# A three-stage kernel on one core: zeros for the places past the first 384 of each expert only, 8 transfers in place of 24

## The chip, the cores and the metric

One core of a Trainium2 chip. The time is device microseconds (us) of one execution of the whole program; lower is better. The engines are TensorE (PE: matmuls; PEld: its weight loads), VectorE (DVE), ScalarE (ACT), GpSimd (POOL) and SyncE (SP). SP and POOL issue the DMA transfers of this kernel, each on a queue of its own; 16 DMA engines carry both.

## What is computed

Attention with landmarks, then a dense feed-forward layer, then a layer of eight experts of which each token takes two. Cut to what matters:

```python
# attention: q, k, v are (4, 8, 576, 64); 32 landmarks are means over 18 rows
A, Bm, C = sm(q, k_lm), sm(q_lm, k_lm), sm(q_lm, k)
Z = ...                      # six steps towards the inverse of Bm
x = (A @ Z @ C @ v)          # laid out as (2304 tokens, 512)
# feed-forward
h = x @ w_in                 # (2304, 2048)
x = (h * np.tanh(np.log1p(np.exp(h)))) @ w_out
# experts
noisy = x @ w_gate + np.log1p(np.exp(x @ w_noise)) * noise
top2 = np.argpartition(-noisy, 2, axis=1)[:, :2]     # with softmax weights top2_w
for e in range(8):
    for k in range(2):
        mask = top2[:, k] == e
        out[mask] += top2_w[mask, k, None] * (np.maximum(x[mask] @ w1[e], 0) @ w2[e])
```

## The kernel before

**Stages.** Attention goes by the 4 batches (`attention`). The feed-forward layer goes by 8 units of 288 tokens, two to a batch. A unit has 8 steps (`hidden`): 12 matmuls into `ps_h` (L733), the nonlinear function on ACT and DVE (among it L753, L763 and L771 on DVE), and 24 matmuls with `w_out` into `ps_acc` (L788 to L790). Since `w_in` is folded into the attention's small matrices (`fold`, L700), batch b's units need batch b's attention, whose last step on TensorE is L568. While a batch's units run, the next batch's attention runs between them: `kT` and `qT` are loaded and summed to landmarks `kl` and `ql` by DVE (L327), multiplied on TensorE (L356, L390), transposed (L470, L474), multiplied with `v` (L486) and put through six small steps (L548).

**Routing.** When a unit is done, `route` copies it to `yT` (ACT), computes the gate (36 pairs of matmuls, L866 before and L864 after the change), finds each token's two experts and its place in each, and scatters the token's row (512 values and 4 of bookkeeping, 2064 bytes) to `slots` in DRAM (L1012, POOL). Each expert has a list of `CAP` = 640 places there: a first part of `CAPA` = 384 and a second of `CAPB` = 256. The expert stage then loads blocks of 128 places (`gather`), 384 or 256 to a job, multiplies them and adds the results to `out` by the token's number. For a place past the expert's count the number is set out of bounds (`entries`, L1082), so nothing is written for it.

**The zeros.** `zeros` waits until the third step of unit 0 is planned (`downed[2]`), clears a tile `zero` and writes it over all 8 x 640 places by DMAs on POOL's queue (`fill`, L282), in three sets: places 0 to 287, 288 to 575 and 576 to 639 of each expert, 8 transfers to a set. After each set an event `filled[i]` is set, and the routing of units 0, 1 and 2 waits for one each in the plan. Later it clears `out` with six more transfers. On the chip, the scatters wait for the fills that stand ahead of them, as both write `slots`.

**What sets the order.** Every engine and queue does its instructions in the order in which they are written. That order comes from a planner that runs while the kernel is built (`Order`): the parts are generators that ask for an engine with a cost, for a transfer with its bytes, or wait for events; an engine takes, of the requests that are ready, the one with the earliest due time (`DU`). The planner keeps one clock for all transfers, so bytes taken away move the planned times of all later loads, and with them the order on every engine.

**Other traffic.** While unit 0 runs, SP loads, in the order of the plan: `w_out` in pieces of 512 KB (`raw`, split by DVE in L599 to L603 and L662, two buffers in turn, so that a piece is asked for when DVE is done with the one two before), `win` (parts of `w_in` for the next batch's fold), `kT`, `qT` and the two pieces of `v`.

Of the kernel before, what the change touches and what calls it, by code (L numbers as in the profile page):

```python
# [19 lines left out]
NTOK, D = 2304, 512  # L20
DFF, NE, DFE = 2048, 8, 1024
U = 288
# [4 lines left out]
CAPA, CAPB = 384, 256  # L27
CAP = CAPA + CAPB
# [3 lines left out]
LW = 4  # L32
# [154 lines left out]
def op(engine, cost, late=0.0):  # L187
    return ("op", engine, cost, late)


def wait(event):
    return ("wait", event)


def get(ring, n=1):
    return ("get", ring, n)
# [18 lines left out]
class Kern:  # L215
# [589 lines left out]
    def zeros(self):  # L805


        yield wait(self.downed[2])
        tk = yield get(self.r_raw)
        zero = self.wp.tile([128, D + LW], F32, name="zero", tag="raw", bufs=2)  # L810
        yield op("V", 0.2)
        self.V.memset(zero, 0.0)
        slots = self.slots[: NE * CAP].rearrange("(e c) x -> e c x", e=NE)
        for i, c in enumerate(range(0, CAP, U)):
            n = min(U, CAP - c)
            for e in range(NE):
                dst = slots[e, c : c + n].rearrange("(n p) x -> p n x", p=min(n, 96))
                src = zero[: min(n, 96)].unsqueeze(1).broadcast_to([min(n, 96), max(n // 96, 1), D + LW])
                yield from self.fill(dst, src, n * 4 * (D + LW))
            self.o.set(self.filled[i])  # L820
        yield wait(self.downed[20])
        rows = self.out.rearrange("(p n) x -> p n x", p=128)
        for n in range(0, NTOK // 128, 3):
            yield from self.fill(rows[:, n : n + 3], zero[:, :D].unsqueeze(1).broadcast_to([128, 3, D]), 786432)
        self.o.put(self.r_raw, tk)
        self.o.set(self.zeroed)

    def route(self, u, acc, ta):
# [25 lines left out]
        sent, rr, trr = Event(), [], []  # L854
        o.spawn(send(), due_hidden(8 * u + 7) + DU["send"])
        yield wait(self.routed[u - 1] if u else self.emptied)
        if u < len(self.filled):
            yield wait(self.filled[u])
        tg = yield get(self.r_g)
        lg = self.bank()  # L860
        yield op("T", 0.9)
        for b in range(3):
            for c in range(4):
                for q in range(3):  # L864
                    n = 32 * (3 * b + q)
# [404 lines left out]
    def run_all(self):  # L1270
# [13 lines left out]
        self.got_wo, self.upped, self.downed = events(range(NF)), events(range(nh)), events(range(nh))  # L1284
        self.folded, self.emptied, self.zeroed, self.x_open, self.y_open, self.m_open, self.last_h = (Event() for _ in range(7))
        self.routed_a = Event()
        self.filled = [Event() for _ in range(0, CAP, U)]
        self.AT, self.WT, self.win, self.gt = {}, {}, {}, {}
        for name in ("AT", "WT", "win", "gt", "mw", "x", "yp"):
            setattr(self, "t_" + name, {})  # L1290
# [87 lines left out]
        def now(gen):  # L1378

            try:  # L1380
                while True:
                    next(gen)
            except StopIteration as r:
                return r.value


        with last:
            n_it = nc.values_load(self.nrounds[0:1, 0:1], min_val=0, max_val=(NROUND - 1) * NE)  # L1388
            with tc.For_i(0, n_it) as i:
                for p, n in ((0, CAPA), (1, CAPB)):  # L1390
                    row = i * CAP + (NE * CAP + p * CAPA)
                    of = lambda t: t.rearrange("p r e -> p (r e)")[:, bass.ds(i, 1)]
                    lw, off, _ = now(self.entries(row, p * CAPA // 128, n // 128, of(self.exps), of(self.left), "x%d" % p))
                    x = now(self.gather(row, n, Event()))
# [61 lines left out]
```

## Time and profile before

| | us |
|---|---|
| three runs | 962.16, 966.08, 966.98 |
| median | 966.08 |
| profiled execution | 968.66 |
| its span, first to last instruction | 966.8 |
| TensorE busy in it | 914.0 |
| POOL busy in it | 136.4 |

The profile records one execution. A busy TensorE is work in flight: matmuls follow each other at shorter distances than a single one lasts. The profile names for each idle time what ended it. Transfers show as issues (on SP's or POOL's queue) and as the share of the 16 DMA engines that each queue's packets took; in that view q1 is SP's queue and q0 is POOL's. The rows on which the prediction rests stand further below.

### The profile page before, as it was taken

The page shows a single profiled execution, that of the slowest core. Times are in us where ns is not written, and L with a number is a line of the kernel's source. Part 1 is how long each engine was busy: PE and PEld are TensorE (multiplying, and loading weights), DVE is VectorE, ACT ScalarE, POOL GpSimd, SP SyncE. Part 2 cuts the span into 40 slices and gives each one's busy share as a digit, 9 for nine tenths or more (in the row PEclk, how much of TensorE's full clock was granted, in tenths as well). Part 3 has the DMA queues.
Part 4 walks back from the last instruction along what each step waited for, and adds up shares of the span by engine and source line. Part 5 has one row for each costly group of instructions (what it writes and reads, how often), then busy time and mean ns, then how long its engine had stood idle before and what let it go on. Part 6 is the DMA issues. An engine that isn't in the chain of part 4 may idle for free. (4 is left out here: it accounts for less than half of the span.)

```text
span 966.8 us, 18134 instructions
## 1 busy us (share of the span) xinstructions
PE 914.0 (95%) x7135; PEld 799.1 (83%) x7135; DVE 625.7 (65%) x1519; ACT 457.6 (47%) x825; POOL 136.4 (14%) x129
## 2 busy tenths in 40 slices
PE   9979768999999998999999989999999999999995
PEld 7767656878886877889898979899989899999984
DVE  6999689566986669486958466646565555445411
ACT  2247655667766686588853233333333223323210
POOL 0002100223101200202020412101121011111102
PEclk9989989999999999999999999999999999999998
DMA  8677950565406410323243667666556355464103
GB/s 303 198 256 255 360 209 3 152 192 173 194 7 200 164 53 2 115 67 86 58 153 91 153 191 162 148 169 143 135 118 158 109 111 125 98 165 94 17 3 51
DMA packets 70075, 131.62 MB, mean 136 GB/s; under 512 B 13696, under 2 KB 34784, under 8 KB 69984
## 3 DMA queue, kind: packets, MB, share of 16 engines
q1 hardware_dynamic: 56960, 96.16, 32.6%
q0 software_dynamic: 13024, 34.25, 15.1%
q8 instruction: 58, 0.95, 0.4%
q14 instruction: 33, 0.27, 0.1%
HBM read 91.94 MB, written 39.48 MB: 136 GB/s over the span
## 5 line engine op out<-in xcount | busy, mean ns | idle before, releaser
L1151 PE MATMUL ps_up<-xh,mw 128*128 128x256 f32 (+1 forms) x1024 | 265.5, 312 | 2.8 <-ACT mw L1039 2.1
L1151 PEld LDWEIGHTS ps_up<-xh,mw 128*128 128x128 f32 x1024 | 183.1, 189 | 15.5 <-ACT mw L1039 2.5
L1160 ACT ACTIVATE gh<-ps_up 128x384 fp32r<-128x384 f32 (+1 forms) x128 | 56.1, 438 | 285.7 <-PE ps_acc L1173 161.6
L1162 DVE SCALAR_TENSOR_TENSOR gl<-ps_up,gh 128x384 fp32r<-128x384 f32 (+1 forms) x128 | 62.7, 490 | 170.1 <-ACT gh L1160 169.9
L788 PE MATMUL ps_acc<-gh,wo 128*128 128x288 f32 x512 | 159.2, 311 | 5.3 <-ACT gh L768 5.0
L1151 PE MATMUL ps_up<-xl,mw 128*128 128x384 f32 (+1 forms) x512 | 159.3, 311 | 0.0
L789 PE MATMUL ps_acc<-gl,wo 128*128 128x288 f32 x512 | 153.2, 299 | 2.8 <-DVE gl L771 2.8
L790 PE MATMUL ps_acc<-gh,wo 128*128 128x288 f32 x512 | 152.7, 298 | 0.2 <-DVE wo L662 0.2
L733 PE MATMUL ps_h<-ah,gt 128*128 128x288 f32 x512 | 127.3, 306 | 15.7 <-ACT mh L746 15.2
L1172 PE MATMUL ps_acc<-mw,gh 128*128 128x512 f32 x320 | 126.5, 395 | 0.0
L1173 PE MATMUL ps_acc<-mw,gh 128*128 128x512 f32 x320 | 126.4, 395 | 0.0
L1174 PE MATMUL ps_acc<-mw,gl 128*128 128x512 f32 x320 | 125.8, 393 | 0.0
L1185 POOL DMA_INDIRECT out<-yp,off x40 | 67.0, 1674 | 376.9 <-DVE yp L1181 278.3
L788 PEld LDWEIGHTS ps_acc<-gh,wo 128*128 128x128 f32 x512 | 97.9, 191 | 25.5 <-issue 13.2
L733 PEld LDWEIGHTS ps_h<-ah,gt 128*128 128x128 f32 x512 | 90.0, 191 | 32.5 <-ACT mh L746 21.5
L1151 PEld LDWEIGHTS ps_up<-xl,mw 128*128 128x128 f32 x512 | 96.7, 189 | 10.0
L789 PEld LDWEIGHTS ps_acc<-gl,wo 128*128 128x128 f32 x512 | 98.0, 191 | 3.8 <-DVE gl L771 3.8
L1041 DVE TENSOR_TENSOR mw<-mraw,mw 128x1024 fp32r<-128x1024 f32 x72 | 87.8, 1223 | 18.5 <-ACT mw L1039 17.9
L790 PEld LDWEIGHTS ps_acc<-gh,wo 128*128 128x128 f32 x512 | 97.9, 191 | 0.4 <-DVE wo L662 0.4
L1012 POOL DMA_INDIRECT slots<-rr,sl x48 | 47.7, 994 | 336.4 <-DVE rr L1008 319.4
L1039 ACT CAST mw<-mraw 128x1024 fp32r<-128x1024 f32 x72 | 74.6, 1042 | 3.4 <-DMA mraw<-in_ew 3.4
L733 PE MATMUL ps_h<-al,gt 128*128 128x288 f32 x256 | 76.0, 297 | 0.0
(189 smaller groups left out, 1384.9 us busy)
## 6 DMA issues: line engine op xcount, KB each, us to landing
mraw<-in_ew SPq DMA_DIRECT2D x72, 512.0 KB, 4.1
win<-win_d SPq DMA_DIRECT2D x48, 256.0 KB, 3.4
xg<-slots SPq DMA_DIRECT2D x160, 64.0 KB, 3.1
slots<-zero POOLq DMA_DIRECT2D x16, 580.5 KB, 20.0
raw<-in_w_in SPq DMA_DIRECT2D x16, 512.0 KB, 4.7
raw<-in_w_out SPq DMA_DIRECT2D x16, 512.0 KB, 6.3
kT<-in_kT SPq DMA_DIRECT2D x8, 576.0 KB, 6.9
qT<-in_qT SPq DMA_DIRECT2D x8, 576.0 KB, 7.3
```

The costliest lines, as they stand in the source:

```text
L733: T.matmul(hp[:, i, :U], gt[:, x, hg, n : n + 128], AT[y][:, hg, :], start=k == 0, stop=k == 5)
L788: T.matmul(acc[c][:, :U], hi[:, n], gh[:, i], start=f + i == 0, stop=False)
L789: T.matmul(acc[c][:, :U], hi[:, n], gl[:, i], start=False, stop=False)
L790: T.matmul(acc[c][:, :U], lo[:, n], gh[:, i], start=False, stop=f + i == NF - 1)
L1039: self.A.copy(w[:, 0], raw)
L1041: self.V.tensor_tensor(out=w[:, 1], in0=raw, in1=w[:, 0].bitcast(F32), op=OP.subtract)
L1151: T.matmul(h[:, :n], w[:, i, 128 * c : 128 * c + 128], x[j][:, c, :n], start=k == 0, stop=k == 11)
L1162: self.V.scalar_tensor_tensor(out=gl[:, :n], in0=hp[:, :n], scalar=0.0, in1=gh[:, :n].bitcast(F32), op0=OP.max, op1=OP.subtract)
L1172: T.matmul(a, g[0][:, n], w[:, 0, 512:], start=first, stop=False)
L1173: T.matmul(a, g[0][:, n], w[:, 1, 512:], start=False, stop=False)
L1174: T.matmul(a, g[1][:, n], w[:, 0, 512:], start=False, stop=last)
L1185: st = self.G.indirect_dma_start(out=self.out[:, :], out_offset=bass.IndirectOffsetOnAxis(ap=off[:, b : b + 1], axis=0), in_=y, in_offset= ...
```

## The change

Only the second part of each expert's list, places 384 to 639, is filled: one transfer for each expert, 128 partitions with two places each, 8 in all. There is one event `filled` now, and the routing of unit 0 alone waits for it in the plan. Places below 384 to which no token was scattered keep what was in DRAM; their results are written nowhere, as before.

```diff
--- before.py
+++ after.py
@@ -811,13 +811,11 @@
         yield op("V", 0.2)
         self.V.memset(zero, 0.0)
         slots = self.slots[: NE * CAP].rearrange("(e c) x -> e c x", e=NE)
-        for i, c in enumerate(range(0, CAP, U)):
-            n = min(U, CAP - c)
-            for e in range(NE):
-                dst = slots[e, c : c + n].rearrange("(n p) x -> p n x", p=min(n, 96))
-                src = zero[: min(n, 96)].unsqueeze(1).broadcast_to([min(n, 96), max(n // 96, 1), D + LW])
-                yield from self.fill(dst, src, n * 4 * (D + LW))
-            self.o.set(self.filled[i])
+        slots = slots[:, CAPA:].rearrange("e (n p) x -> e p n x", p=128)
+        for e in range(NE):
+            src = zero.unsqueeze(1).broadcast_to([128, CAPB // 128, D + LW])
+            yield from self.fill(slots[e], src, CAPB * 4 * (D + LW))
+        self.o.set(self.filled)
         yield wait(self.downed[20])
         rows = self.out.rearrange("(p n) x -> p n x", p=128)
         for n in range(0, NTOK // 128, 3):
@@ -854,8 +852,8 @@
         sent, rr, trr = Event(), [], []
         o.spawn(send(), due_hidden(8 * u + 7) + DU["send"])
         yield wait(self.routed[u - 1] if u else self.emptied)
-        if u < len(self.filled):
-            yield wait(self.filled[u])
+        if u == 0:
+            yield wait(self.filled)
         tg = yield get(self.r_g)
         lg = self.bank()
         yield op("T", 0.9)
@@ -1284,7 +1282,7 @@
         self.got_wo, self.upped, self.downed = events(range(NF)), events(range(nh)), events(range(nh))
         self.folded, self.emptied, self.zeroed, self.x_open, self.y_open, self.m_open, self.last_h = (Event() for _ in range(7))
         self.routed_a = Event()
-        self.filled = [Event() for _ in range(0, CAP, U)]
+        self.filled = Event()
         self.AT, self.WT, self.win, self.gt = {}, {}, {}, {}
         for name in ("AT", "WT", "win", "gt", "mw", "x", "yp"):
             setattr(self, "t_" + name, {})
```

The planner's order changes with it. On POOL 14 fills, then 2, then 8 small ones become 8 in one piece. Three more places follow. In the rows, a name behind the line is the instruction's output, its input and the shape.

SP's queue, the loads of unit 0's last pieces of `w_out` and of batch 1's second half (`kT`, `qT`). Before:

```order
L287 DMA raw<-in_w_out 128x1024
L287 DMA win<-win_d 128x512
L287 DMA raw<-in_w_out 128x1024
L287 DMA kT<-in_kT 128x1152
L287 DMA qT<-in_qT 128x1152
L287 DMA win<-win_d 128x512
L287 DMA raw<-in_w_out 128x1024
```

and now:

```order
L287 DMA raw<-in_w_out 128x1024
L287 DMA win<-win_d 128x512
L287 DMA raw<-in_w_out 128x1024
L287 DMA win<-win_d 128x512
L287 DMA kT<-in_kT 128x1152
L287 DMA qT<-in_qT 128x1152
L287 DMA raw<-in_w_out 128x1024
```

One `win` has moved ahead of `kT` and `qT`; the rest stands as it was, two rows later or earlier.

DVE, from the reduction to `ql` of batch 1's second half on (L361 takes the maximum of the product of L356; `raw` in L599 is a piece of `w_out`). Before:

```order
L327 TENSOR_REDUCE ql<-qT 128x64
L771 SCALAR_TENSOR_TENSOR gl<-mh,gh 128x576
L662 TENSOR_TENSOR wo<-t,wo 128x512
L763 SCALAR_TENSOR_TENSOR mh<-me,mh 128x576
L361 TENSOR_REDUCE mxC<-ps_g 128x1
L599 TENSOR_SCALAR raw<-raw 128x512
L361 TENSOR_REDUCE mxC<-ps_g 128x1
L601 SCALAR_TENSOR_TENSOR raw<-raw 128x512
L364 TENSOR_SCALAR nb<-mxC 128x1
L603 SCALAR_TENSOR_TENSOR raw<-raw 128x512
```

and now:

```order
L327 TENSOR_REDUCE ql<-qT 128x64
L771 SCALAR_TENSOR_TENSOR gl<-mh,gh 128x576
L662 TENSOR_TENSOR wo<-t,wo 128x512
L763 SCALAR_TENSOR_TENSOR mh<-me,mh 128x576
L599 TENSOR_SCALAR raw<-raw 128x512
L753 TENSOR_SCALAR me<-mh 128x576
L361 TENSOR_REDUCE mxC<-ps_g 128x1
L601 SCALAR_TENSOR_TENSOR raw<-raw 128x512
L361 TENSOR_REDUCE mxC<-ps_g 128x1
L603 SCALAR_TENSOR_TENSOR raw<-raw 128x512
```

The first step on the next `raw` (L599) and a step of `hidden` (L753) now stand ahead of the first L361.

TensorE, where batch 1's first half is transposed and the gate of unit 0 is computed. Before:

```order
L470 MATMUL ps_g<-ident,EC 128x128 x4
L733 MATMUL ps_h<-ah,gt 128x288
L733 MATMUL ps_h<-al,gt 128x288
L733 MATMUL ps_h<-ah,gt 128x288 x2
L733 MATMUL ps_h<-al,gt 128x288
L733 MATMUL ps_h<-ah,gt 128x288
L474 MATMUL ps_g<-ident,EC 64x128
L866 MATMUL ps_g<-wgn,yT 32x16 x36
L486 MATMUL ps_g<-vt,CT 32x64 x20
```

and now:

```order
L470 MATMUL ps_g<-ident,EC 128x128 x4
L864 MATMUL ps_g<-wgn,yT 32x16 x36
L474 MATMUL ps_g<-ident,EC 64x128
L788 MATMUL ps_acc<-gh,wo 128x288
L789 MATMUL ps_acc<-gl,wo 128x288
L790 MATMUL ps_acc<-gh,wo 128x288
L788 MATMUL ps_acc<-gh,wo 128x288
L789 MATMUL ps_acc<-gl,wo 128x288
L790 MATMUL ps_acc<-gh,wo 128x288
L486 MATMUL ps_g<-vt,CT 32x64 x20
```

The gate's matmuls have come ahead of L474, directly behind the first transposes, and matmuls of the next unit (L788 to L790) stand where `ps_h` was computed.

## Rows read from the trace of the kernel before

**Rows 1.** The page: busy us of each engine, share of the span, instructions.
```profile
PE 914.0 (95%) x7135; PEld 799.1 (83%) x7135; DVE 625.7 (65%) x1519; ACT 457.6 (47%) x825; POOL 136.4 (14%) x129
```

**Rows 2.** Table by stretches: us of each engine's work, PEclk, DMA share, GB/s.
```profile
100.00:120.00 20.00, 13.93 (x121) 11.43 (x119) 12.66 (x25) 13.41 (x28) 3.34 (x5) 0.99 1.02 351
120.00:140.00 20.00, 12.25 (x85) 10.24 (x86) 16.32 (x30) 11.08 (x21) 0.00 (x0) 0.76 0.70 268
140.00:160.00 20.00, 13.68 (x244) 11.03 (x243) 18.77 (x50) 11.40 (x26) 0.00 (x0) 1.00 0.01 2
180.00:200.00 20.00, 20.00 (x150) 16.99 (x149) 8.12 (x13) 13.83 (x22) 8.38 (x13) 1.00 0.68 202
200.00:220.00 20.00, 18.07 (x185) 14.67 (x184) 15.15 (x38) 12.64 (x26) 0.53 (x1) 0.91 0.56 178
```

**Rows 3.** Timeline of TensorE: start us, us, instruction [idle before <-releaser].
```profile
104.43 1.17 PE L356 MATMUL ps_g<-kT,ql 64*32 64x288 f32 x16
...
113.74 0.29 PE L788 MATMUL ps_acc<-gh,wo 128*128 128x288 f32 x1
113.87 0.29 PE L789 MATMUL ps_acc<-gl,wo 128*128 128x288 f32 x1
...
123.25 0.61 PE L733 MATMUL ps_h<-ah,gt 128*128 128x288 f32 x1 [7.77 <-ACT mh L746]
...
132.56 1.65 PE L356 MATMUL ps_g<-kT,ql 64*32 64x288 f32 x16 [4.50 <-DVE ql L327]
...
144.06 0.63 PE L470 MATMUL ps_g<-ident,EC 128*128 128x128 f32 x4 [2.12 <-DVE rB L511]
...
151.61 0.65 PE L470 MATMUL ps_g<-ident,EC 128*128 128x128 f32 x4 [2.59 <-DVE z L877]
```

**Rows 4.** Timeline of DVE.
```profile
112.68 0.46 DVE L753 TENSOR_SCALAR me<-mh 128x576 f32<-128x576 f32 x1
118.77 0.43 DVE L599 TENSOR_SCALAR raw<-raw 128x512 int32<-128x512 int32 x1 [5.63 <-DMA raw<-in_w_out]
119.12 0.75 DVE L763 SCALAR_TENSOR_TENSOR mh<-me,mh 128x576 f32<-128x576 f32 x1
...
124.29 0.43 DVE L599 TENSOR_SCALAR t<-raw 128x512 int32<-128x512 int32 x1 [0.56 <-DMA raw<-in_w_out]
...
127.56 1.35 DVE L327 TENSOR_REDUCE kl<-kT 128x64 f32<-128x1152 f32 x1 [1.20 <-DMA kT<-in_kT]
...
131.15 1.35 DVE L327 TENSOR_REDUCE ql<-qT 128x64 f32<-128x1152 f32 x1 [1.64 <-DMA qT<-in_qT]
...
134.80 0.43 DVE L599 TENSOR_SCALAR raw<-raw 128x512 int32<-128x512 int32 x1
```

**Rows 5.** DMA queues: packets, MB, share; 105 to 115 us, then 85 to 111.
```profile
q0 software_dynamic: 770, 2.87, 91.4%
q1 hardware_dynamic: 168, 0.41, 10.3%
...
q0 software_dynamic: 1150, 4.31, 47.2%
```

**Rows 6.** Timeline of the queue of SP (issues).
```profile
108.52 0.33 SPq L287 DMA_DIRECT2D raw<-in_w_out  x1
...
116.90 1.77 SPq L287 DMA_DIRECT2D win<-win_d  x1
123.76 0.33 SPq L287 DMA_DIRECT2D raw<-in_w_out  x1
```

**Rows 7.** The page: DMA issues, KB each, median us to landing.
```profile
raw<-in_w_out SPq DMA_DIRECT2D x16, 512.0 KB, 6.3
...
qT<-in_qT SPq DMA_DIRECT2D x8, 576.0 KB, 7.3
```

**Rows 8.** Timeline of POOL: the first scatter and the second burst.
```profile
176.33 1.01 POOL L1012 DMA_INDIRECT slots<-rr,sl  x1 [63.62 <-DVE rr L1008]
...
184.34 0.72 POOL L282 DMA_DIRECT2D slots<-zero  x1 [2.83 <-DMA slots<-rr,sl]
```

## The prediction

> **What bounds the kernel now.** I read the busy times first: TensorE works 914.0 of 966.8 us [rows 1]. So the kernel is bound by TensorE nearly everywhere, and a transfer matters only where TensorE stops. The table by stretches shows where [rows 2]: of the 60 us from 100 to 160, TensorE is busy 13.93 + 12.25 + 13.68 = 39.86, so 20.1 us are idle there, while the DMA engines are full from 100 to 120 (share 1.02). From 180 to 200, in the second burst of fills, it is busy for all 20.00 us.
>
> TensorE's own rows name the idle pieces [rows 3]: 7.77 us before 123.25, 4.50 before 132.56, then 2.12 before 144.06 and 2.59 before 151.61. The first two end in ACT and in DVE's `ql`. DVE's rows say what those waited for [rows 4]: at 118.77 DVE had stood 5.63 us for `raw`, a piece of `w_out`; then 0.56 for the next `raw`, 1.20 for `kT` and 1.64 for `qT`. DVE takes its work in order, so behind the late `raw` stood the softplus step (L763) that ACT and TensorE needed, though its own input was there. These are four waits for loads, 9.03 us together.
>
> The DMA view says why the loads are late [rows 5]. Q0 is POOL's queue (fills), q1 is SP's (loads). From 105 to 115 the fills take 91.4% of the engines' time and the loads 10.3%. The `raw` issued at 108.52 [rows 6] was taken up by DVE at 118.77, over 10 us later, where the median of such loads in the whole run is 6.3 us [rows 7].
>
> **The change, part by part.** *Bytes.* Before: 16 fills of 288 x 2064 bytes and 8 of 64 x 2064, 10.57 MB; now 8 of 256 x 2064 bytes, 4.23 MB. The first burst was 14 fills of 594,432 bytes, 8.32 MB. Now it is the 4.23 MB alone, issued at the same place. Until 111 q0 had moved 4.31 MB [rows 5], so the new burst is over at about 111, and what came after 111 falls to the loads alone.
>
> *Term 1, DVE's waits for loads.* DVE's and SP's rows up to the places shown above are the same but for a few neighbours that changed places, and `raw` is issued at 108.52 as before. With the queue free from 111 I give it the run's median of 6.3 us: landed at 114.8. DVE was ready at 112.68 + 0.46 = 113.14 [rows 4], so a wait of 1.7 us stays where 5.63 was. From 118.77 to 131.15 DVE took 12.38 us, 3.40 of them waits for the other three loads; without these, 8.98. So the reduction to `ql` starts at 114.8 + 8.98 = 123.8 instead of 131.15. `qT` must be there by then: SP now issues a `win` ahead of it, and even if each issue still takes as long as in the crowded stretch, `qT` goes out where that `win` did, at 116.90 [rows 6], and lands 7.3 us later [rows 7], at 124.2; with short issues at 121. I count no wait. That is a **gain of 7.35**. Bounds: 9.0 if `raw` is there at 113.14; 3.4 if its 5.63 stay, since that load goes out while the fills still run.
>
> The DMA share is where a rule and the trace differ: q1 got a tenth in 105 to 115 [rows 5]. The Trainium skill (DMA: Bandwidth & Descriptors, section Queues, rings and completion order) says that each DMA engine goes round between the queues that have work, packet by packet; by that the loads would have had about half, `raw` would now be there when DVE wants it, and the sum would be 1.7 us larger. The trace shows less than half, so I keep the 1.7 as a wait.
>
> *Term 2, the new order from there to batch 1's last step.* Counted over the order, 24 more matmuls of L788 to L790 stand ahead of batch 1's L568 than before (294 for 270), and DVE does one more L763 and L771 ahead of its L559. From 140 to 160 DVE is busy 18.77 of 20 us [rows 2] while TensorE has the gaps of 2.12 and 2.59 and two smaller ones, 20.00 - 13.68 = 6.3 us. So DVE sets the pace there and matmuls put into gaps are free: 24 x 0.13 us (starts of neighbours, [rows 3]) = 3.1 us that need not be done later, against 2 x 0.75 us of DVE (L763's row in [rows 4]; L771 has the same shape) = 1.5. **Gain 1.6.** Bounds: +6.3 if the gaps close, -6.3 if the new order makes them twice as long.
>
> *Term 3, the clock.* After the 7.77 us of idle time the 16 matmuls of L356 at 132.56 took 1.65 us, where the same 16 at 104.43 took 1.17 [rows 3]; the granted clock averages 0.76 over that stretch [rows 2], so part of it ran at the lower of the two levels (1.2 of 2.4 GHz). They stand between `ql` and DVE's L361. If TensorE does not stop for that long it stays at its upper level: **gain 0.5**, or 0.
>
> *Term 4, what costs nothing.* The second burst, the last 2 large and the 8 small fills, from 184.34 on [rows 8], lay beside a TensorE busy for all of 180 to 200; from 200 to 220 it misses 1.93 us [rows 2]. Value 0, bound +1.9. POOL: 16 issues fewer; the first scatter at 176.33 waited 63.62 us for DVE, not for a fill [rows 8], so no one is helped by POOL being free. Behind batch 1 the order differs on into batch 2 (18 of the matmuls of L788 to L790 fewer ahead of its L568) and has the same counts again at batch 3's, so the work itself nets to 0; I allow 1.9 us either way, the idle time of 200 to 220, for waits that come or go. If the cover of term 4, a full TensorE, were gone, the second burst would cost what the first did per byte; but it is not there any more.
>
> **Sum.** 7.35 + 1.6 + 0.5 = 9.45 us. Check from DVE: it works 12.66 + 16.32 + 18.77 = 47.75 us from 100 to 160 [rows 2]; at the share of 140 to 160 (0.94) that needs 50.8 us, so some 9.2 can go, and never more than 12.25. The profiled execution took 968.66 us, so the changed one should take 959.2; the median of the runs, 966.08, lies 2.6 below it, and against that the forecast is **956.6 us**.
>
> **Rivals.** *A: a wait takes the place of the old one.* DVE's L599 on the last `raw` now stands ahead of both L361, as the order shows. That `raw` was issued 4.99 us after DVE took the earlier one [rows 4, 6]; less the 0.56 of wait, it goes out now at 114.8 + 4.43 = 119.2. DVE comes to it 3.2 us after `ql` begins (3.65 less the L361 that moved), at 127.0. At 6.3 us it lands at 125.5, in time. At the 11.04 us that it took before (123.76 to 134.80) it lands at 130.2: 3.2 us lost in the chain, 959.8. For it: the `v` loads follow at once. Against: no fill is left. Chance 0.12.
>
> *B: no change that can be told.* The time won before 132 is lost again at the handovers of 140 to 160: DVE has to stay 94% busy over the whole stretch, where it managed 0.80 from 100 to 160. If half or more of term 1 is lost and term 2 is nothing, 3.7 us or less remain: 962.4 to 966. Against: nothing in the rows ties what follows to a fixed time; TensorE is busy for all of 180 to 200. Chance 0.15. The Trainium skill (Perfetto Trace Analysis, section Identifying the Most-Contended Engine) says to look for the engine with the highest occupancy and to work on that one first; by that rule alone fewer fills would leave the time at 966. The stretches above speak against it here.
>
> *C: slower.* In the new order the 36 matmuls of L864 (routing, unit 0) stand right behind the first L470 of batch 1 and ahead of L474. They need all four copies to `yT` on ACT, and TensorE holds everything behind them, the whole chain to L568. That decides if the wait there exceeds the gain: with term 1 and 3 worth 7.85, it must pass 12.7 us to make the kernel slower by over 0.5%. The gaps of that chain are 6.3 us now; at three and a half times that, 15.8 more, the time is 966.1 - 7.85 + 15.8 = 974.0. For it: TensorE already stops at that place. Against: no single wait in it is over 2.59 [rows 3]. Chance 0.06.
>
> *D: more.* The gaps close as well, 12.25 from DVE's bound and the 1.9: 952. Chance 0.06. That the change doesn't do what it says is settled by the order: 8 fills of 128x2x516 stand there. Rows of `slots` that are no longer cleared are still loaded and multiplied, with equal counts.
>
> **How the numbers follow.** The forecast has 0.61. A measurement can tell about 0.5%, 4.8 us, from no change. Faster by more: forecast, A and D, 0.79; within: B, 0.15; slower: C, 0.06. All bounds at once would reach from 950 (12.25 + 1.9 + 1.9) to 971 (3.4 - 6.3 - 1.9, a loss of 4.8). The upper end needs every term to fail together, so I stop inside B, whose lower half is in: 950 to 963.5, with C and the rest of B, less than 0.2, left out.
>
> **What would show it.** Right: q0 moves 4.2 MB between 85 and 140 and is done near 111; DVE's wait for `raw` near 113 is under 2 us and those for `kT` and `qT` are gone; TensorE's idle time from 100 to 160 falls from 20 to about 11 us and the clock there does not drop to half; everything from 180 on is the same, some 9 us earlier. Wrong: DVE's wait for `raw` stays at 5 us (term 1), L361 comes late behind L599 (A), TensorE's gaps at L470 to L548 grow (B, C), or waits come up between 200 and 400.

## The result and the profile after

| | before | after |
|---|---|---|
| runs | 962.16, 965.48, 966.08, 966.98 | 953.30, 953.31, 953.32, 957.34 |
| median | 965.78 | 953.32 |
| profiled execution | 968.66 | 957.34 |
| its span | 966.8 | 955.5 |

The changed kernel takes 0.9888 of the time, with a 95% interval of 0.9851 to 0.9924: 12.5 us less by the medians and 10.8 by that ratio, where 9.45 were forecast. The execution that was profiled is the longest of the four after, by 4.0 us. The tail of the program is in it too, 2.2 us longer than before (its section comes last). Unless another kernel is named, the rows are from this profile.

TensorE's busy time is what it was (914.0 us in [rows 1]); the table by stretches answers to [rows 2]. The page's line on TensorE, and the table:

```profile
PE 916.5 (96%) x7135; PEld 800.9 (84%) x7135; DVE 625.0 (65%) x1519; ACT 457.1 (48%) x825; POOL 126.1 (13%) x113
```

```profile
100.00:120.00 20.00, 16.12 (x124) 13.16 (x123) 17.68 (x35) 15.91 (x31) 0.00 (x0) 0.91 0.90 322
120.00:140.00 20.00, 16.28 (x190) 13.00 (x190) 17.23 (x42) 14.48 (x30) 0.00 (x0) 0.92 0.18 68
140.00:160.00 20.00, 18.23 (x227) 15.50 (x225) 17.17 (x48) 10.96 (x23) 0.00 (x0) 0.83 0.01 2
180.00:200.00 20.00, 20.00 (x212) 16.81 (x213) 13.91 (x23) 16.60 (x30) 0.00 (x0) 1.00 0.58 194
200.00:220.00 20.00, 19.93 (x155) 16.44 (x153) 15.86 (x53) 10.39 (x20) 1.11 (x2) 1.00 0.33 113
```

From 100 to 160 TensorE is busy 16.12 + 16.28 + 18.23 = 50.63 of 60 us, so it idles 9.4 where it idled 20.1. The DMA share from 120 to 140 is 0.18, where it was 0.70. The clock is the one thing there that did not come as forecast: 0.91, 0.92 and 0.83.

The queues of SP (q1) and POOL (q0), 105 to 115 us and then 85 to 111, answer to [rows 5]; the issues on SP's queue to [rows 6]:

```profile
q1 hardware_dynamic: 751, 2.32, 69.5%
q0 software_dynamic: 339, 1.20, 33.8%
```

```profile
q0 software_dynamic: 1152, 4.23, 41.6%
```

```profile
106.35 0.33 SPq L287 DMA_DIRECT2D raw<-in_w_out  x1
106.77 0.38 SPq L287 DMA_DIRECT2D win<-win_d  x1
...
109.66 0.43 SPq L287 DMA_DIRECT2D kT<-in_kT  x1
110.14 0.42 SPq L287 DMA_DIRECT2D qT<-in_qT  x1
```

All 4.23 MB of fills have gone by 111, as forecast, and the loads have 69.5% of the ten microseconds in which they had a tenth. The issues themselves are short now: 0.33 to 0.43 us for `raw`, `win`, `kT` and `qT`, where `win` at 116.90 and its neighbours took 1.7 to 2.4. DVE's timeline answers to [rows 4]:

```profile
110.88 0.46 DVE L753 TENSOR_SCALAR me<-mh 128x576 f32<-128x576 f32 x1
112.52 0.43 DVE L599 TENSOR_SCALAR raw<-raw 128x512 int32<-128x512 int32 x1 [1.18 <-DMA raw<-in_w_out]
...
119.37 1.34 DVE L327 TENSOR_REDUCE kl<-kT 128x64 f32<-128x1152 f32 x1
...
121.23 1.34 DVE L327 TENSOR_REDUCE ql<-qT 128x64 f32<-128x1152 f32 x1
...
126.23 0.42 DVE L599 TENSOR_SCALAR raw<-raw 128x512 int32<-128x512 int32 x1
...
126.93 0.45 DVE L361 TENSOR_REDUCE mxC<-ps_g 128x1 f32<-128x288 f32 x1
...
127.90 0.45 DVE L361 TENSOR_REDUCE mxC<-ps_g 128x1 f32<-128x288 f32 x1
```

One wait for a load is left, 1.18 us for `raw` at 112.52; `kl` and `ql` start without one, and the next `raw` (126.23), ahead of both L361, is there in time. TensorE, to be read against [rows 3]:

```profile
116.99 0.61 PE L733 MATMUL ps_h<-ah,gt 128*128 128x288 f32 x1 [3.16 <-ACT mh L746]
...
123.05 1.18 PE L356 MATMUL ps_g<-kT,ql 64*32 64x288 f32 x16
...
135.28 0.40 PE L733 MATMUL ps_h<-ah,gt 128*128 128x288 f32 x1 [1.72 <-ACT mh L746]
```

The gap of 7.77 us is 3.16 now, the one of 4.50 ahead of L356 is gone, one of 1.72 stands at 135.28, and the 16 matmuls of L356 take 1.18 us instead of 1.65.

### The profile page after: what moved, and what is told of

Its sections match the earlier page's. It is cut to its first block, busy times and chain, and to the rows that moved or that the text cites. A ratio compares the mean times of both kernels' runs of the same rounds, so it can differ in the third digit from the quotient of the medians.

```text
span 955.5 us, 18095 instructions
## 1 busy us (share of the span) xinstructions
PE 916.5 (96%) x7135; PEld 800.9 (84%) x7135; DVE 625.0 (65%) x1519; ACT 457.1 (48%) x825; POOL 126.1 (13%) x113
## 5 line engine op out<-in xcount | busy, mean ns | idle before, releaser
L788 PE MATMUL ps_acc<-gh,wo 128*128 128x288 f32 x512 | 160.1, 313 | 5.5 <-ACT gh L768 3.5
L790 PE MATMUL ps_acc<-gh,wo 128*128 128x288 f32 x512 | 153.0, 299 | 0.7 <-DVE wo L662 0.7
L788 PEld LDWEIGHTS ps_acc<-gh,wo 128*128 128x128 f32 x512 | 98.1, 192 | 27.3 <-issue 15.3
L790 PEld LDWEIGHTS ps_acc<-gh,wo 128*128 128x128 f32 x512 | 98.0, 191 | 1.4 <-DVE wo L662 1.4
```

The source lines that it names most:

```text
L788: T.matmul(acc[c][:, :U], hi[:, n], gh[:, i], start=f + i == 0, stop=False)
L790: T.matmul(acc[c][:, :U], lo[:, n], gh[:, i], start=False, stop=f + i == NF - 1)
```

## The experiments

They ran on other chips than the first pair. On these the kernel before takes 977.4 to 977.5 us (e1 to e10) or 972.8 (e11 and e12), so ratios are compared, always to the kernel before on the same chip. Four marks of each profile say where its time lies: from batch 1's first `kl` to its second `ql` on DVE (the loads), from there to the first gate matmul of unit 1 on TensorE (the chain and the order), TensorE's gaps in that gate, and the tail, from the issue of the last scatter into `out` to the end of the span.

| kernel | ratio, 95% interval | `kl` to `ql` | `ql` to gate | gaps in it | tail |
|---|---|---|---|---|---|
| before, first chip | 1 | 31.95 | 70.37 | 3 x 0.62 | 9.69 |
| after, first chip | 0.9888 (0.9851 to 0.9924) | 23.24 | 70.81 | none | 11.93 |
| e1: old order, new bytes | 0.9934 (0.9915 to 0.9952) | 22.56 | 70.50 | 3 x 0.62 | 12.13 |
| e2: new order, old bytes | 0.9924 (0.9907 to 0.9941) | 28.71 | 66.91 | none | 9.03 |
| e3: new order, half the bytes | 0.9871 (0.9851 to 0.9892) | 21.97 | 66.91 | none | 11.83 |
| e4: old order, first burst alone | 0.9977 (0.9960 to 0.9995) | 30.60 | 70.34 | 3 x 0.62 | 8.63 |
| e5: after again | 0.9892 (0.9868 to 0.9917) | 23.57 | 66.92 | none | 11.85 |
| e6: before again | 1 | 32.68 | 70.65 | 3 x 0.62 | 9.09 |
| e7: later fills, 4.23 MB | 0.9858 (0.9831 to 0.9885) | 22.26 | 64.56 | none | 12.27 |
| e8: later fills, 10.57 MB | 0.9827 (0.9799 to 0.9855) | 22.06 | 64.52 | none | 9.12 |
| e9: before with later fills | 0.9993 (0.9974 to 1.0012) | 22.11 | 60.84 | 1 x 0.62 | 9.20 |
| e10: e7 in half rows | 0.9801 (0.9775 to 0.9826) | 22.26 | 64.53 | none | 8.85 |
| e11: after in half rows | 0.9912 (0.9888 to 0.9936) | 24.84 | 67.48 | none | 9.16 |
| e12: after again | 0.9927 (0.9902 to 0.9951) | 24.41 | 67.50 | none | 12.24 |

**e1 and e2: bytes and order apart.** The change does two things at once, so each ran alone. e1 keeps the plan of before, and with it every engine's order, while only the eight transfers of the change are sent:

```diff
-        self.nc.gpsimd.dma_start(dst, src)
+        if dst is not None:
+            self.nc.gpsimd.dma_start(dst, src)
...
+                dst = None if i else slots[e, CAPA:].rearrange("(n p) x -> p n x", p=128)
+                src = zero.unsqueeze(1).broadcast_to([128, CAPB // 128, D + LW])
```

> The plan, and with it the order on PE, DVE, ACT and SP, is that of the kernel before; only the transfers on POOL are those of the change (8 fills of the places 384 to 639, 4.23 MB, at the place of the first 8). If the loads held back by the fills are the whole cause: the full gain, 953 to 954 (12 us less than 966). If the loads give the gain up to ql (8.7 us, 9.9 less the 1.2 by which that execution was ahead before the first fill) and the new order gives the rest: 957 to 958, with TensorE's 1.9 us of gaps at unit 1's gate matmuls and the lower clock behind them still there. If the order is the cause: 966.

Measured: 0.9934, 6.5 us of 977, between the second and the third case of the expectation. No DVE wait for a load is left, and the way to `ql` is as short as with the whole change. The gaps at the gate are there as before, and the tail is 3.0 us longer than in e6, which the expectation didn't have: the 6.5 us are what is left after that loss. They also hold what the missing second burst is worth (e4).

e2 keeps the order of the change and writes about the bytes of the old first burst: places 128 to 639, 8.45 MB.

```diff
-        slots = slots[:, CAPA:].rearrange("e (n p) x -> e p n x", p=128)
+        slots = slots[:, 128:].rearrange("e (n p) x -> e p n x", p=128)
...
-            src = zero.unsqueeze(1).broadcast_to([128, CAPB // 128, D + LW])
+            src = zero.unsqueeze(1).broadcast_to([128, 4, D + LW])
```

> The order of the change, with twice the bytes in its 8 fills (places 128 to 639 of each expert, 8.45 MB where the first burst of before had 8.32). Loads as the cause: DVE's wait for raw near 113 is 4 to 6 us again, kT and qT are late again, and 8 to 9 us of the gain are gone: 961 to 963. Order as the cause: 953 as with the change.

Measured: 0.9924, 7.4 us, which lies between the two expectations (0.995 to 0.997 and 0.987). It isn't the order alone: e2 also sends no second burst, and 8 large fills in place of 14. Against e4 below, with the old order, no second burst and 8.32 MB, it takes 5.2 us less by the ratios: that is the order, with the form of the fills. DVE's waits for loads in this profile (in total, times, longest, us):

```profile
DVE raw L599 <- DMA raw<-in_w_out: 2.8, 1, 2.8
DVE kl L327 <- DMA kT<-in_kT: 2.7, 1, 2.7
DVE ql L327 <- DMA qT<-in_qT: 0.9, 1, 0.9
```

They come to 6.4 us, where e4 has 7.9: the bytes cost most of what they cost before. The gain lies in the first column (28.71, in e4 30.60), where no run parts the order from the form of the fills, in the second, 66.91 for 70.34, and in the third. There the old order has gaps in unit 1's gate. TensorE and ACT in e4, which has the old order and no second burst, and the same place in e2:

```profile
197.60 0.25 PE L866 MATMUL ps_g<-wgn,yT 128*32 128x16 f32 x6
198.47 0.25 PE L866 MATMUL ps_g<-wgn,yT 128*32 128x16 f32 x6 [0.62 <-ACT yT L839]
199.34 0.25 PE L866 MATMUL ps_g<-wgn,yT 128*32 128x16 f32 x6 [0.62 <-ACT yT L839]
```

```profile
197.16 0.38 ACT L839 COPY yT<-ps_acc 128x288 f32<-128x288 f32 x1
197.44 0.68 ACT L755 ACTIVATE me<-me 128x576 f32<-128x576 f32 x1
198.03 0.39 ACT L839 COPY yT<-ps_acc 128x288 f32<-128x288 f32 x1
198.31 0.69 ACT L757 ACTIVATE me<-me 128x576 f32<-128x576 f32 x1
198.89 0.39 ACT L839 COPY yT<-ps_acc 128x288 f32<-128x288 f32 x1
```

```profile
192.56 0.94 PE L864 MATMUL ps_g<-wgn,yT 128*32 128x16 f32 x72
```

In the old order ACT takes turns between the copies to `yT` and the steps of the nonlinear function (L755, L757), each gate matmul waits for its copy, and TensorE stands three times 0.62 us. In the new order all four copies precede (the last at 191.37) and the gate goes through in one piece. In the profile of before the granted clock from 205 to 210, behind these gaps, was 0.68 and the matmuls started 0.24 us apart instead of 0.13: another 5 x 0.32 = 1.6 us. All four profiles with the old order (before, e1, e4, e6) have the gaps, none with the new one has. The low clock is not in all four: 0.51 from 195 to 200 in e1 and 0.78 from 205 to 210 in e6, but 1.00 from 200 to 210 in e4.

**e3 and e4: fewer bytes still, and the second burst.** e3 fills only places 512 to 639 (2.11 MB) in the order of the change; e4 has the old order, the 14 transfers of the first burst (8.32 MB) and none of the second.

```diff
# e3
-        slots = slots[:, CAPA:].rearrange("e (n p) x -> e p n x", p=128)
+        slots = slots[:, 512:].rearrange("e (n p) x -> e p n x", p=128)
# e4
+                dst = None if 8 * i + e > 13 else slots[e, top - U : top].rearrange("(n p) x -> p n x", p=96)
+                src = zero[:96].unsqueeze(1).broadcast_to([96, 3, D + LW])
```

> The order of the change with fills of the last 128 places of each expert alone, 2.11 MB. Loads as the cause: DVE's last wait for raw near 112 (1.2 us) goes too, 952 to 953. If bytes counted in proportion to the 6.3 MB taken away already (12.5 us): 949.

> The order of the kernel before and its first burst (14 fills, 8.32 MB, which here cover the places 352 to 639 of all experts and 64 to 351 of six), without the second burst (the other 2 and the 8 small ones, 2.25 MB). If the second burst costs nothing, as the prediction had it: 966, and TensorE's gaps near 202 stay. If it was what held unit 1's routing and the clock: 962 to 963.

Measured: 0.9871 and 0.9977. With e3 the last wait of DVE goes, but `ql` comes only 1.6 us sooner than in the change (21.97 for 23.57): most of what bytes can give was had by the change. The second burst, which the prediction priced at 0 with a bound of 1.9, is worth 2.3 us here by the times (interval 0.5 to 3.9). Where they go isn't shown: the profile of e4 is 2.1 us ahead of e6's at `ql` already, before the second burst starts. The gaps at the gate stay, so these belong to the order and not to the burst.

**e5 to e8: the place of the fills.** If a fill costs only by the loads that it meets, it is enough to send it when the loads are done. e5 and e6 are the two kernels once more. e7 lets `zeros` wait for `downed[6]` in place of `downed[2]` and moves unit 0's wait for `filled` from ahead of its gate to ahead of its scatters; e8 is e7 with all 640 places, 10.57 MB.

```diff
# e7, against the change
-        yield wait(self.downed[2])
+        yield wait(self.downed[6])
...
-        if u == 0:
-            yield wait(self.filled)
...
         V.tensor_copy(rr[0][:, :, D:], en)
+        if u == 0:
+            yield wait(self.filled)
# e8, against e7
-        slots = slots[:, CAPA:].rearrange("e (n p) x -> e p n x", p=128)
+        slots = slots.rearrange("e (n p) x -> e p n x", p=128)
...
-            src = zero.unsqueeze(1).broadcast_to([128, CAPB // 128, D + LW])
+            src = zero.unsqueeze(1).broadcast_to([128, CAP // 128, D + LW])
```

> The changed kernel as it is, beside the two that follow and beside the kernel before, so that all stand on one chip. Theory (the time went from the stretch between the first fill and unit 1's gate, by waits for loads and by the order): ratio to the kernel before 0.985 to 0.992; in the profile no DVE wait for a load over 1.5 us between 95 and 160, and TensorE busy for at least 19.5 of the 20 us before unit 1's gate. Rival (a good part of the 12.5 us was the state of that one chip): ratio 0.993 or more.

> The kernel before, for a second profile on the chip of the other runs. If the gaps of TensorE at unit 1's gate (three of 0.6 us near 203) and the low clock behind them belong to the old order, they are there again and the stretch is 1.5 to 2 us short of full; if they were an accident of one execution, it is full. If the stall at the last step of batch 2 (about 280 us), which four profiles of changed kernels showed, belongs to those kernels, it is absent here; if it belongs to the chip, it is here too.

> The eight fills of the change, but planned behind the seventh of unit 0's eight steps instead of behind the third, so that they start when DVE comes to the reductions of batch 1's second half (near 120 us) and few loads are left; unit 0's routing waits for them only ahead of its scatters. Theory (what the fills of the change still cost is contention with the loads at 87 to 111 us: a DVE wait of 1.2 us for raw, and a gap of TensorE of 3.2 us with a low clock behind it): the wait is gone, TensorE idles 2 us or less from 100 to 120, and the ratio to the kernel before lies 0.2 to 0.6 per cent below that of the change in the same runs. Rival one (nothing is left to win there): the same ratio within 0.15 per cent. Rival two (the later fills meet the v loads and the last raw, and the chain to L568 is late): 0.3 per cent or more above that of the change.

> As the run before this one, with all 640 places of each expert filled (10.57 MB, as the kernel before moves, in eight transfers). Theory (a fill costs only by the loads that it meets, not by its bytes): near 120 us the queue has next to nothing else to do, so the 10.57 MB cost at most 2 us more than the 4.23 MB at the same place, and the kernel is faster than the one before by 0.8 per cent or more with not a byte less to move. Rival (bytes count wherever they are): the 6.3 MB more cost 6 us or more against the run before this one, as the same bytes did when the old order was kept.

Measured: e7 0.9858 and e8 0.9827, beside 0.9892 for the change. e8 moves as many bytes as the kernel before and is the faster by 1.7%. Its table by stretches, and POOL's queue from 111 to 170:

```profile
100.00:120.00 20.00, 17.58 (x145) 14.58 (x144) 19.29 (x38) 16.18 (x32) 4.57 (x5) 1.00 0.62 203
120.00:140.00 20.00, 17.18 (x238) 13.26 (x236) 17.22 (x44) 11.49 (x26) 2.73 (x4) 1.00 1.02 378
140.00:160.00 20.00, 18.43 (x238) 15.84 (x239) 19.00 (x59) 15.71 (x31) 0.00 (x0) 1.00 0.49 179
```

```profile
q0 software_dynamic: 2752, 10.77, 49.2%
```

The DMA engines are full from 120 to 140 (share 1.02) and TensorE is busy for 17.18 us there, where it is 16.28 in the change with 4.23 MB and a queue that is mostly empty. e7 and e8 agree to 0.2 us in the first two columns with 6.3 MB between them: up to the gate, bytes are free at this place. In the old places, the second burst's included, the 6.3 MB cost 6.5 us (e1). DVE has no wait for a load in either. Both rivals of e7 (nothing left to win; `v` late) lie outside, though its interval and that of the change overlap, and TensorE idles 2.4 us from 100 to 120, not 2 or less. e8 lies 2.1 us below e7 by the medians (the intervals overlap), and its tail is 3.1 us shorter; so apart from the tail its bytes cost about 1 us, less than these runs can tell. The stall near 280 us that was asked of e6 is in both kernels on that chip (DVE 3.8 us in e6, 4.5 in e5, at L571), so it doesn't belong to the change.

**e9: the place alone, with 24 transfers.** The two edits of e7 in the kernel before, where units 0 to 2 each wait for their set ahead of their scatters.

```diff
-        yield wait(self.downed[2])
+        yield wait(self.downed[6])
...
-        if u < len(self.filled):
-            yield wait(self.filled[u])
...
         V.tensor_copy(rr[0][:, :, D:], en)
+        if u < len(self.filled):
+            yield wait(self.filled[u])
```

> The kernel before with its 24 fills and all of its 10.57 MB, and with two waits of the plan moved: the fills are planned behind the seventh step of unit 0 instead of the third, and the routing of units 0 to 2 waits for them ahead of its scatters instead of ahead of its gate. Theory (neither the bytes nor the number of the fills cost anything, only that they meet the loads at 87 to 125 us): it gains about what the two kernels with later fills gained, a ratio of 0.982 to 0.989, with no DVE wait for a load from 95 to 135 us. Rival one (the number of transfers counts, since a POOL issue and a set each hold the plan): a ratio of 0.990 to 0.997. Rival two (scatters and fills that now alternate on POOL's queue make unit 0 to 2's routing late): 0.997 or more.

Measured: 0.9993, so the theory as written there falls and rival two stands. `ql` and the gate come as early as in e7 or earlier; then it is lost. POOL's timeline and a row of DVE's, and the table by stretches:

```profile
166.33 1.00 POOL L1012 DMA_INDIRECT slots<-rr,sl  x1 [42.02 <-DVE rr L1006]
167.63 0.96 POOL L1012 DMA_INDIRECT slots<-rr,sl  x1 [0.30 <-issue]
172.02 0.72 POOL L282 DMA_DIRECT2D slots<-zero  x1 [3.43 <-DMA slots<-rr,sl]
176.67 0.94 POOL L1012 DMA_INDIRECT slots<-rr,sl  x1 [3.93 <-DMA slots<-zero]
...
186.17 4.83 POOL L282 DMA_DIRECT2D slots<-zero  x7 [4.91 <-DMA slots<-rr,sl]
213.29 0.96 POOL L1012 DMA_INDIRECT slots<-rr,sl  x1 [22.29 <-DVE rr L1006]
216.39 0.58 POOL L282 DMA_DIRECT2D slots<-zero  x1 [2.15 <-DMA slots<-rr,sl]
221.25 0.95 POOL L1012 DMA_INDIRECT slots<-rr,sl  x1 [4.28 <-DMA slots<-zero]
```

```profile
186.01 0.57 DVE L851 STREAM_TRANSPOSE rr<-yT 32x384 f32<-32x384 f32 x1 [3.24 <-DMA slots<-rr,sl]
```

```profile
180.00:200.00 20.00, 17.20 (x186) 14.37 (x185) 14.16 (x28) 11.47 (x23) 5.79 (x9) 1.00 0.84 268
200.00:220.00 20.00, 14.51 (x114) 10.71 (x111) 13.00 (x46) 9.57 (x19) 1.54 (x2) 0.91 0.53 172
220.00:240.00 20.00, 16.91 (x143) 12.54 (x142) 13.80 (x29) 11.89 (x26) 9.92 (x13) 1.00 0.55 158
```

Nine fills go out from 115 to 124; the other 15 come between scatters. A scatter waits for the fill ahead of it and a fill for the scatter ahead of it, 2.0 to 4.9 us each time, DVE waits 3.24 us for unit 0's scatters before it may write the next unit's rows, and TensorE idles 2.80 + 5.49 + 3.09 = 11.4 us from 180 to 240, where e6 idles 2.2. That these waits are what takes the gain back is read from the rows; the order on the other engines is another as well, and no run parts the two. What is shown is that moving the fills is not enough: 24 of them did not fit ahead of the scatters in the plan, eight did.

**e10 to e12: the tail.** By then the last column had split in two groups (8.6 to 9.7 and 11.8 to 12.3 us), so e10 and e11 send each fill as two transfers of half a row: same bytes, twice the elements, in e7's place and in that of the change. e12 is the change beside e11. Between e11 and e12 the order differs on POOL alone.

```diff
+            half = (D + LW) // 2
+            self.nc.gpsimd.dma_start(slots[e][:, :, :half], src[:, :, :half])
-            yield from self.fill(slots[e], src, CAPB * 4 * (D + LW))
+            yield from self.fill(slots[e][:, :, half:], src[:, :, half:], CAPB * 4 * (D + LW))
```

> The kernel with eight later fills of 4.23 MB, each fill now written as two transfers of half a row: the same bytes and places, 4096 elements of 1032 bytes instead of 2048 of 2064. It asks about the end of the program: from the issue of the last scatter into out to the end of the span, the five kernels that filled 4.23 MB or less took 11.8 to 12.3 us, the five that filled 8.3 MB or more 8.6 to 9.7, though the same work stands there. If that goes with the number of elements that POOL's queue has carried, the tail is 8.5 to 10 us here; if with the bytes, 11.5 to 12.5. The rest should be as with the eight whole fills: ratio 0.983 to 0.989.

> The changed kernel with each of its eight fills written as two transfers of half a row, in the same place on POOL's queue: 4096 elements of 1032 bytes instead of 2048 of 2064; the order on all other engines is the same. Theory (the end of the program is shorter by some 3 us when POOL's queue has carried 4000 elements of fills or more): from the issue of the last scatter into out to the end of the span 8.6 to 9.7 us instead of 11.8 to 12.3, and a ratio 0.2 to 0.4 per cent below that of the changed kernel in the same runs. Rival (the short tail came with the later fills or with the bytes): a tail of 11.5 or more and no difference over 0.15 per cent. The smaller elements may also make the fills longer while the loads are out (87 to 111 us): then DVE's wait for raw grows from 1.2 to 1.5 us to 3 or more and part of the gain is lost there.

> The changed kernel again, as the partner of the run before this one on the same chip. Ratio to the kernel before 0.987 to 0.992; tail from the last issue 11.8 to 12.3 us; if the tail differs by 2 us or more from execution to execution of the same program, it is 9 us here and the theory of the elements falls.

Measured: tails of 8.85 and 9.16 against 12.24, as the theory of the elements had it. The last issue in e11 and in e12, with spans of 963.5 and 964.3 us:

```profile
954.34 1.54 POOL L1185 DMA_INDIRECT out<-yp,off  x1 [0.56 <-DVEq L1389]
```

```profile
952.06 1.54 POOL L1183 DMA_INDIRECT out<-yp,off  x1 [0.56 <-DVEq L1387]
```

But e11 comes to that issue 2.28 us later: 0.43 us at `ql` (DVE's wait for `raw` is 2.8 instead of 2.4) and most of the rest early in the expert stage, between the first and the seventh scatter into `out` (63.61 us instead of 62.12), which I can't tell the cause of. Net the ratio is 0.0015 below e12's, less than forecast, and the intervals overlap: a shorter tail is shown, a faster changed kernel is not. e10, at 0.9801 with an interval that ends at 0.9826, below the 0.983 to 0.989 expected, is the fastest kernel of the study, about 0.9% below the change by the ratios on their chips.

## Why the prediction was right, and which terms were not

The sign, the range and the place were right, but the sum came out near for a partly wrong reason: three terms were too small, and a loss at the end of the program was not in it. The pair e6 and e5, both from one chip (the second chip, below), gives the account. From the kernel before to the change, `kl` to `ql` is 9.1 us shorter and `ql` to the gate 3.7; by the last L568, of batch 3, the lead over the first fill has grown to 15.7; the expert stage gives 0.8 back and the tail 2.8, which makes 12.1, and the spans differ by 12.0. That what was missed on both sides nearly cancels is luck, and the size itself is only known as 7 to 12.5 us: by the medians 12.5, 10.8 (e5) and 6.9 (e12).

- **What bounds it, right.** TensorE is busiest everywhere, yet the time came from the stretch with the idle 20 us, now 9.4 (11 forecast). The Trainium skill (Perfetto Trace Analysis, section Identifying the Most-Contended Engine) would start at the engine with the highest occupancy. That is TensorE here, and the time did come from TensorE's gaps; but its sum says nothing of them (914.0 and 916.5 us of work in spans of 966.8 and 955.5), and what made them were DVE's waits for loads and the order on ACT.
- **Term 1, waits for loads: right in mechanism, 1.4 us too small.** 7.35 forecast, 8.7 on the first chip and 9.1 on the second; e1 shows it alone. The time to land was right: `raw` issued at 106.35 was taken at 112.52, 6.17 us later (6.3 assumed). What the step had wrong is "`raw` is issued at 108.52 as before": measured from the first fill (88.56 and 87.35) it went out 1.0 us sooner. SP asks for it when DVE is done with the buffer (L662, which ends at 108.49 and 106.32), and DVE is ahead because in the new order ACT does L761 ahead of L746 and DVE's L763 waits less for it; before and after:

```profile
103.21 0.76 DVE L763 SCALAR_TENSOR_TENSOR mh<-me,mh 128x576 f32<-128x576 f32 x1 [1.40 <-ACT me L761]
```

```profile
100.98 0.76 DVE L763 SCALAR_TENSOR_TENSOR mh<-me,mh 128x576 f32<-128x576 f32 x1 [0.38 <-ACT me L761]
```

So this 1.0 us belongs to the order: from the first fill to this issue it is 19.95 us in e1 (old order, new bytes) and 18.99 in e2 (new order, old bytes). The rest is DVE's 8.71 us to `ql` in place of 8.98.
- **The wait that was kept: right in size, wrong in its reason.** 1.7 us forecast; 1.18, 1.5 (e5) and 2.4 (e12) measured. The Trainium skill (DMA: Bandwidth & Descriptors, section Queues, rings and completion order) has the engines go round between queues with work, packet by packet. The prediction read the loads' 10.3% from 105 to 115 against that; where both queues are at work the finer rows agree with it: in the kernel before, from 116 to 120, loads move 241 packets and fills 240. The 10.3% has another cause. The loads' queue had little left when the `raw` of 108.52 was issued, and from then to 112.0 it moved 4 packets while the fills moved 294. From 112 to 115 it moved 54 against 179, and only from then on as many. So the load came late by a late start, not by a small share (the last section has the rows). e2's 25.7% from 105 to 115 (fills 76.3%) is the same: no packet up to 109.0, and from 109.5 on as many as the fills.
- **Term 2, the order: mis-sized.** 1.6 forecast, for 3.1 of matmuls less 1.5 of DVE's work. From `ql` to the gate the second chip shows 3.7, and e2 against e1 3.6 (66.91 and 70.50), as if DVE's 1.5 us were not paid; no run shows them by themselves. In the first pair this column doesn't move (70.37 and 70.81), and the profiled execution of the change has a fall of the clock of its own there (0.54 from 150 to 155, 0.78 to 160), which e5 doesn't have (1.00): 5 x 0.46 + 5 x 0.22 = 3.4 us, about what is missing.
- **Term 3, the clock: the 0.5 came, the claim behind it did not.** L356 takes 1.18 us instead of 1.65, but the clock still fell behind the gap of 3.16: 0.63 from 115 to 120 and 0.69 to 125. In e5 it was 1.00 there, behind a gap of 3.48.
- **Term 4 and the later order: wrong at 0.** "TensorE busy for all of 180 to 200" was read as cover; the idle 1.93 us of 200 to 220 [rows 2] were known and left as a bound. They are the three gaps at unit 1's gate, and the low clock behind them adds 1.6; with the new order on ACT both are gone. e4 gives the second burst another 2.3 us; which work it delays was not found.
- **Not in the sum: the tail**, 2.2 to 2.8 us longer with the change.
- **Rivals.** A fell: no wait at L599 ahead of L361. C fell: the gate of unit 0 behind L470 brings no gap of TensorE over 0.92 us from 137 to 160 (0.85 here, 0.92 in e5). B fell with the ratio. D is half true: the gaps of 140 to 160 close in e5 to 1.9 us and in e12 to 0.4.

## What to carry to other kernels

Price a background transfer by the loads that it meets, not by its bytes: taking 6.3 MB out of the old places was worth 6.5 us (e1), and putting them back 30 us later costs nothing that the runs can tell (e8 against e7). Before taking bytes away, look for a stretch in which the queue is idle, and send the transfer there in one piece, ahead of whatever waits for it (e8 against e9). And where a planner's order hangs on planned bytes, run the order and the bytes apart: here the bytes alone were worth 6.5 us and the order about 5 (e2 against e4), of which the trace of before shows three gaps of 0.62 us on an engine that was called full.

## What the runs showed of the hardware beside that

- **The tail goes with the elements that POOL's queue has carried.** Counting the contiguous rows that the fills write, eight profiles have 4032 to 5120 of them (before, e2, e4, e6, e8 to e11) and a tail of 8.6 to 9.7 us, six have 1024 or 2048 (after, e1, e3, e5, e7, e12) and one of 11.8 to 12.3. Neither bytes nor transfers sort them so: e10 and e11 have the 4.23 MB of the long tails, e2 and e8 their eight transfers. The packets of the last scatter end within 5 us of its issue in e11 and in e12, so the 3 us pass when hardly anything moves any more. Why is open.
- **Two queues share by packets, but a load beside many fills starts late.** Packets, MB and share of the 16 engines, where both queues have work:

| kernel, stretch (us) | loads, q1 | fills, q0 |
|---|---|---|
| before, 116 to 120 | 241, 0.67, 42.2% | 240, 0.88, 59.9% |
| after, 100 to 104 | 256, 0.73, 45.7% | 257, 0.95, 57.8% |
| e2, 116 to 120 | 252, 0.68, 42.5% | 254, 0.98, 59.9% |

From the issue of the `raw` that DVE waits for to the first half microsecond in which its queue moves more than 2 packets it is 3.5 us in before, 3.8 in e6, 3.7 in e2 and e4, 3.1 in e12, and 1.2 in the profile of the change, where the fills thin out from 107.5. In e7, with no fills out, it is 0.7. Behind the late start of before, e4 and e6 the loads first move some 8 packets in half a microsecond beside some 25 of the fills; in e2 they don't. Why is open.
- **Issues take longer beside the fills of before.** An issue of `win`, `kT` or `qT` holds SP's queue 1.7 to 2.4 us in the fills' stretch of before, 1.6 to 2.6 in e4 and 0.38 to 0.43 after. Full DMA engines alone don't do it: in e2 the share is 1.03 from 100 to 125, and the same issues take 0.45 to 0.87. What about the 14 fills does is open.
- **Chips differ by about 1%** for the same kernel (965.8, 972.8 and, on three chips, 977.4 to 977.5 us), and the ratio of the change with them: 0.9888, 0.9927 and 0.9892, intervals overlapping.
